# A Strassen unit in tile 1, two key selections side by side, and key sums behind the last values, in a fused attention and feed-forward kernel

## The chip, the core and the metric

One core of a Trainium2 chip. The metric is the device time of one execution in microseconds (us); a kernel is timed in several runs and the median is quoted. Ratios are computed as the mean time of one kernel's fast runs over the mean of the other's fast runs of the same rounds, so they are not quite the ratios of the medians. A run more than 1.5% above the fastest of its kernel counts as slow and is left out of the ratio. The span of a profile (first to last instruction) is about 1.8 us shorter than the timed execution that it belongs to.

Engines: PE is the tensor engine, DVE the vector engine, ACT the scalar engine, POOL is GpSimd, SP only issues transfers here. A *bank* is one of the eight result buffers that PE writes; before PE starts another result in it, this program lets it wait until DVE or ACT have read ("evicted") the old one.

## The reference, cut to what matters

```python
# q, k, v: (8 batches, 8 heads, 576, 64); 4608 tokens, 512 -> 2048 -> 512
k_p = k.reshape(B, H, 72, 8, D).mean(axis=3)        # pooled keys; values likewise
attn = softmax(q @ k_p.T / 8)
x = (attn @ v_p)                                    # to (4608, 512)
h = x @ w_in
out = (h * sigmoid(h)) @ w_out
```

## The kernel before

The kernel walks over nine tiles of 512 tokens. A tile has an *up* phase (x @ w_in and silu, hidden state transposed in `h_T`) and a *down* phase (the product with `w_out`). Attention for the next batch is cut into small pieces, *fillers*, hung between the matmuls: `f_up.append((22, f))` means that f is emitted after step 22 of the up phase. In the up phase a step is one matmul of 512 columns or a pair of 256.

The up phase has two kinds of work: a *plain* group (four matmuls of 512 columns and one activation), or a *unit*, Strassen's scheme for four groups at once: seven products of four 256-column matmuls, with sums on DVE.

```python
def product(y, n, bank, first):
    if first:
        ps[bank] = ps_tile([128, 2, NQ], FP32, "at", f"u_ps{bank}")   # pool "at": 5 banks, "mm": 3
    w, x = unit_weights(y, n), unit_x(t, n)
    ...                                             # 4 matmuls
def stage(y, n):
    if n == "2":   product(y, 2, "P", True);  nc.scalar.copy(r_sb, ps["P"])
    elif n == "5": product(y, 5, "Q", True);  tt(out=rr_sb, in0=ps["Q"], in1=r_sb, op=ALU.add)
    elif n == "1": product(y, 1, "R", True);  tt(out=t_sb, in0=ps["R"], in1=rr_sb, op=ALU.subtract)
    elif n == "4": product(y, 4, "P", False); hidden(y, 1, 0, ps["P"])
    elif n == "3": product(y, 3, "Q", False); hidden(y, 0, 1, ps["Q"])
    ...
```

The down phase is one such scheme for the whole tile. It needs sums of the hidden state (`hidden_sum`, on DVE) and ends with `o_sb` being evicted from banks P and Q:

```python
def down_quarters(t, fillers, last=False):
    product(2, KA, KQ); product(5, KA, KQ); product(2, 0, KA)      # 2 and 5 read hidden sums
    nc.scalar.copy(r_sb, ps["P"]); product(5, 0, KA)
    tt(out=rr_sb, in0=ps["Q"], in1=r_sb, op=add)
    ...                                             # products 1, 4, 3
    product(7, 0, KQ, cc); tt(out=o_sb[0][:, cs, LO], in0=ps["P"][:, cs], in1=t_sb[:, cs], op=add)
    product(6, 0, KQ, cc); tt(out=o_sb[1][:, cs, HI], in0=ps["Q"][:, cs], in1=t_sb[:, cs], op=add)
```

The attention pieces that the argument touches (shortened):

```python
def pool_k(b, stage):               # from batch 3 on; keys come in two transfers, the second adding
    if stage == 0: add_halves(raw)  # DVE, 72x1024: the first reader of the landed keys
    else: ...                       # DVE, two more sums, to kp
def select_k(b, a): ...             # 12 small PE matmuls into half a of one bank (batches 0 to 2)
def copy_k(b, a):                   # DVE copy of that half to kz
def select_v(b, a): ...             # PE;  copy_v(b, a): DVE copy of half a to vp
def numerators(b, g, f):
    ... lhsT=st["vp"][:, 4 * g + s, c::2] ...       # s in 0..3: half g of vp alone
    nc.vector.tensor_mul(out=xT[...], in0=nu[c], in1=rec)
```

Names in the profile lines: `kp` and `vp` are the pooled keys and values, `kz` the keys as PE reads them; `x_sum`, `w_sum` and `h_sum` are sums of inputs, weights and hidden state; `r_sb`, `rr_sb`, `t_sb` and `c_sb` are the partial sums of a Strassen scheme; `nu_ps` are the numerators.

The softmax here doesn't subtract the row's maximum and nothing guards it: scores larger than these inputs give would overflow.

## Time and profile before

| | before |
|---|---|
| median of the first runs | 294.97 us (294.23 to 295.34) |
| the profiled execution | 293.2 us, span 291.4 us |
| PE / DVE / ACT busy | 97% / 76% / 64% |

The lines are shown in the prediction below. How to read it: PE is busy all through, so time is gained by less work on PE or by fewer of PE's waits, and a wait on PE shows as a start later than the previous start plus 216 ns (512 columns) or 109 ns (256).

For the comparisons I cut the trace at PE's first matmul of each tile (the first `hp_ps` matmul after the last `o_ps` one; where its record is missing, 0.216 us before the next). In the profile before, tile 1 took 33.39 us, tile 2 29.96, tile 3 29.30, and tiles 4, 5, 6 30.31, 29.68 and 30.95.

### The profile page before, as it was taken

The page shows a single profiled execution, that of the slowest core. Times are in us where ns is not written, and L with a number is a line of the kernel's source. Part 1 is how long each engine was busy: PE and PEld are TensorE (multiplying, and loading weights), DVE is VectorE, ACT ScalarE, POOL GpSimd, SP SyncE. Part 2 cuts the span into 40 slices and gives each one's busy share as a digit, 9 for nine tenths or more (in the row PEclk, how much of TensorE's full clock was granted, in tenths as well). Part 3 has the DMA queues.
Part 4 walks back from the last instruction along what each step waited for, and adds up shares of the span by engine and source line. Part 5 has one row for each costly group of instructions (what it writes and reads, how often), then busy time and mean ns, then how long its engine had stood idle before and what let it go on. Part 6 is the DMA issues. An engine that isn't in the chain of part 4 may idle for free. (4 is left out here: it accounts for less than half of the span.)

```text
span 291.4 us, 6563 instructions
## 1 busy us (share of the span) xinstructions
PE 282.9 (97%) x2565; PEld 188.7 (65%) x2585; DVE 222.3 (76%) x408; ACT 187.4 (64%) x400; POOL 52.2 (18%) x68
## 2 busy tenths in 40 slices
PE   8989999989999999999999999999999999999995
PEld 3448434445667676667788767676666666786684
DVE  4986845964889697979598869987888876746783
ACT  1668675558666877588757866786578667425800
POOL 8754216501020012001200107103000000000000
PEclk9999999999999999999999999999999999999999
DMA  7999999993677463954894394978830023004104
GB/s 209 277 279 214 240 290 159 220 208 46 131 104 171 116 102 65 155 153 135 127 182 125 83 150 72 175 149 155 143 91 2 2 54 90 3 0 108 39 2 144
DMA packets 35295, 37.67 MB, mean 129 GB/s; under 512 B 9952, under 2 KB 27616, under 8 KB 35264
## 3 DMA queue, kind: packets, MB, share of 16 engines
q0 software_dynamic: 21760, 20.86, 42.4%
q1 hardware_dynamic: 12928, 15.48, 20.9%
q10 hardware_dynamic: 576, 0.92, 0.9%
q8 instruction: 20, 0.33, 0.5%
q14 instruction: 11, 0.09, 0.1%
HBM read 36.70 MB, written 9.44 MB: 158 GB/s over the span
## 5 line engine op out<-in xcount | busy, mean ns | idle before, releaser
L517 PE MATMUL hp_ps<-xT,w_in_sb 128*128 128x512 bf16 (+3 forms) x413 | 83.6, 340 | 1.9 <-DVE o_sb L653 0.6
L523 ACT ACTIVATE h_T<-hp_ps 128x512 bf16<-128x512 f32 (+2 forms) x99 | 53.7, 548 | 36.7 <-PE hp_ps L517 35.7
L622 PEld LDWEIGHTS <-h_sum 128*128 128x128 bf16 x640 | 60.4, 98 | 15.0 <-issue 6.1
L582 DVE TENSOR_TENSOR h_sum<-h_T 128x1024 bf16<-128x1024 bf16 (+1 forms) x72 | 50.9, 743 | 12.3 <-ACT h_T L523 12.3
L517 PEld LDWEIGHTS <-w_in_sb 128*128 128x128 bf16 x428 | 40.7, 98 | 28.1 <-issue 2.5
L338 ACT ACTIVATE es<-sc_ps 72x288 bf16<-72x288 f32 x128 | 41.3, 402 | 12.6 <-PE sc_ps L330 12.5
L378 DVE TENSOR_TENSOR xT<-nu_ps,rec 128x288 bf16<-128x288 f32 x64 | 25.5, 447 | 8.8 <-PE nu_ps L370 8.8
L459 PEld LDWEIGHTS <-w_sum 128*128 128x128 bf16 x280 | 27.3, 98 | 7.1
L622 PEld LDWEIGHTS <-h_T 128*128 128x128 bf16 x256 | 23.5, 98 | 6.8 <-issue 4.3
L467 ACT ACTIVATE h_T<-c_sb 128x512 bf16<-128x512 f32 x28 | 17.6, 628 | 10.4 <-DVE c_sb L491 10.4
L152 DVE STREAM_TRANSPOSE qT<-q_bf 128x576 bf16<-128x576 bf16 x32 | 23.0, 753 | 0.1
L181 POOL DMA_DIRECT2D raw<-in_k_dram x5 | 7.0, 1404 | 80.5 <-DMA raw<-in_k_dram 39.6
L356 ACT ACTIVATE lnd<-den_ps 128x288 f32<-128x288 f32 x30 | 12.3, 410 | 10.9 <-PE nu_ps L370 5.9
L273 DVE TENSOR_TENSOR raw<-raw 128x384 f32<-128x384 f32 (+3 forms) x20 | 12.4, 619 | 8.1 <-DMA raw<-in_v_dram 4.4
L622 PE MATMUL o_psP<-w_out_sb,h_sum 128*128 128x256 bf16 x128 | 17.6, 273 | 0.0
L622 PE MATMUL o_psQ<-w_out_sb,h_sum 128*128 128x256 bf16 x128 | 17.6, 273 | 0.0
L622 PE MATMUL o_psQ<-w_sum,h_T 128*128 128x256 bf16 x128 | 17.5, 274 | 0.0
L622 PE MATMUL o_psP<-w_sum,h_sum 128*128 128x256 bf16 x128 | 17.0, 273 | 0.0
L622 PE MATMUL o_psR<-w_sum,h_sum 128*128 128x256 bf16 x128 | 16.7, 273 | 0.0
L622 PE MATMUL o_psP<-w_sum,h_T 128*128 128x256 bf16 x128 | 16.7, 273 | 0.0
L187 DVE TENSOR_TENSOR raw<-raw 72x1024 f32<-72x1024 f32 x10 | 12.2, 1215 | 5.0 <-DMA raw<-in_k_dram 5.0
L529 POOL DMA_DIRECT2D out_dram<-o_sb x1 | 0.6, 626 | 83.5 <-issue 83.5
(77 smaller groups left out, 419.9 us busy)
## 6 DMA issues: line engine op xcount, KB each, us to landing
out_dram<-o_sb SPq DMA_DIRECT2D x128, 64.0 KB, 2.5
q_bf<-in_q_dram POOLq DMA_DIRECT2D x6, 576.0 KB, 10.7
raw<-in_k_dram SPq DMA_DIRECT2D x6, 512.0 KB, 5.2
raw<-in_k_dram POOLq DMA_DIRECT2D x5, 576.0 KB, 8.3
raw<-in_v_dram POOLq DMA_DIRECT2D x5, 576.0 KB, 8.6
raw<-in_v_dram SPq DMA_DIRECT2D x5, 512.0 KB, 5.7
w_in_sb<-in_moe_w_in_dram POOLq DMA_DIRECT2D x8, 256.0 KB, 8.6
w_out_sb<-in_moe_w_out_dram POOLq DMA_DIRECT2D x4, 512.0 KB, 13.4
```

Source lines behind the costliest of these rows:

```text
L152: nc.vector.transpose(out=st["qT"][:, a, f * QF : (f + 1) * QF].rearrange("r i c p -> r (i c p)"), in_=st["q_bf"][:, a, f * n : (f + 1) * n],)
L187: nc.vector.tensor_add(out=raw[:, :, : 2 * D], in0=raw[:, :, : 2 * D], in1=raw[:, :, 2 * D :])
L273: nc.vector.tensor_add(out=raw[..., :w], in0=raw[..., :w], in1=raw[..., w : 2 * w])
L338: nc.scalar.activation(es[:, s, :], sc[s], func=AF.Exp, scale=score_scale)
L356: nc.scalar.activation(lnd, den_ps[:, :HS], func=AF.Ln)
L378: nc.vector.tensor_mul(out=xT[:, 2 * g + c, cols], in0=nu[c][:, :HS], in1=rec)
L459: nc.tensor.matmul(ps[bank][:, u, :], lhsT=w[:, kk, 128 * u : 128 * (u + 1)], rhs=x[:, kk, :], start=first and u == 0 and kk == 0, stop=kk ...
L467: nc.scalar.activation(h_T[:, g : g + 2, j * NQ : (j + 1) * NQ], src, func=AF.Silu)
L517: nc.tensor.matmul(hp_ps[:, r0:r1], lhsT=w_in_sb[:, kk, g * 128 : (g + 1) * 128], rhs=xT[:, kk, x0 : x0 + r1 - r0], start=(kk == 0), stop= ...
L523: nc.scalar.activation(h_T[:, g, n0 : n0 + n], hp_ps[:, :n], func=AF.Silu)
L582: nc.vector.tensor_tensor(out=h_sum[n][:, ks, :], in0=quarter(*a, ks), in1=quarter(*b, ks), op=op)
L622: nc.tensor.matmul(ps[b][:, c, :], lhsT=left(n, kt, c), rhs=W_OUT[n][:, kt, :], start=b not in begun, stop=kt == k1 - 1, skip_group_check= ...
```

## The change

Its intent: (a) tile 1 gets one Strassen unit in place of four plain groups, with the weight and x sums moved to suit; (b) the two halves of the key selection of batch 2 stand side by side, with the two copies behind them, so that no selection waits for a copy; (c) the key sums of the next batch go behind the multiply of the last values; (d) bank R of the units moves to the pool of three.

```diff
--- before.py
+++ after.py
@@ -451,7 +451,8 @@
 
         def product(y, n, bank, first):
             if first:
-                ps[bank] = ps_tile([128, 2, NQ], FP32, "at", f"u_ps{bank}")
+                tag = "mm" if bank == "R" else "at"
+                ps[bank] = ps_tile([128, 2, NQ], FP32, tag, f"u_ps{bank}")
             w, x = unit_weights(y, n), unit_x(t, n)
             for u in range(2):
                 next(step)
@@ -768,18 +769,20 @@
         else:
             G = lambda *gs: [(g, 0, NTT) for g in gs]
             if t == 1:
-                items = G(*range(12, 16), *range(4, 12), *range(4))
+                items = (
+                    G(12, 13, 14, 15) + [(0, "251")] + G(8) + [(0, "43")] + G(9)
+                    + [(0, "76")] + G(10) + [(0, "s")] + G(11, 0, 1, 2, 3)
+                )
             else:
                 items = (
                     G(12, 13) + [(0, "251")] + G(14) + [(0, "43")] + G(15) + [(0, "76")]
                     + [(1, "2")] + [(0, "s")] + [(1, "51")] + G(0) + [(1, "43")] + G(1)
                     + [(1, "76")] + G(2) + [(1, "s")] + G(3)
                 )
-            if t > 1:
-                for n in U_X:
-                    f_up.append((0, lambda n=n: unit_x_sum(t, n)))
+            for n in U_X:
+                f_up.append((0, lambda n=n: unit_x_sum(t, n)))
             for n in (2, 5):
-                f_up.append((36, lambda n=n: hidden_sum(n, 4, 8)))
+                f_up.append((36 if t > 1 else 45, lambda n=n: hidden_sum(n, 4, 8)))
             f_up.append((56, lambda: hidden_sum(6, 4, 8)))
             for n, k0 in ((2, 0), (5, 0), (1, 4), (1, 0)):
                 f_up.append((64, lambda n=n, k0=k0: hidden_sum(n, k0, k0 + 4)))
@@ -788,14 +791,14 @@
 
         for n, t0, f_to, at, parts in (
             (1, 0, f_down, 48, (0, PW)), (3, 0, f_down, 52, (0, PW)),
-            (4, 1, f_up, 8, (0, PW)), (7, 1, f_up, 13, (0, PW)),
-            (6, 1, f_up, 40, (0, PW)),
+            (4, 1, f_up, 38, (0, PW)), (7, 1, f_up, 42, (0, PW)),
+            (6, 1, f_up, 60, (0, PW)),
         ):
             for i in range(*parts):
                 if t == t0:
                     f_to.append((at + i, lambda n=n, i=i: weight_sum(n, i)))
         if a < B:
-            q_at = [15, 16, 17, 49] if t else [82, 84, 86, 88]
+            q_at = [15, 16, 17, 49] if t > 1 else [24, 25, 26, 49] if t else [82, 84, 86, 88]
             if t == 0:
                 for j in range(2):
                     f_up.append((44 + 8 * j, lambda j=j: slot_sums("k", j)))
@@ -807,8 +810,8 @@
             elif t == 1:
                 for j in range(2):
                     f_up.append((0, lambda j=j: slot_sums("k", j, halves=True)))
-                    f_up.append((21 + 4 * j, lambda j=j: select_k(2, j)))
-                    f_up.append((21 + 4 * j, lambda j=j: copy_k(2, j)))
+                    f_up.append((22, lambda j=j: select_k(2, j)))
+                    f_up.append((23, lambda j=j: copy_k(2, j)))
                     f_down.append((8, lambda j=j: slot_sums("v", j, halves=True)))
                     f_down.append((40, lambda j=j: select_v(2, j, "at")))
                     f_down.append((41, lambda j=j: copy_v(2, j)))
@@ -828,8 +831,8 @@
                     for n in U_W:
                         f_down.append((6, lambda y=y, n=n: unit_weight_sum(y, n)))
             elif a + 1 < B:
-                f_down.append((80, lambda: pool_k(a + 1, 0)))
-                f_down.append((100, lambda: pool_k(a + 1, 1)))
+                for stage in range(2):
+                    f_down.append((100, lambda stage=stage: pool_k(a + 1, stage)))
                 f_up.append((0, lambda: load_q(a + 1)))
                 f_up.append((1, lambda: load_one(a + 1, "k")))
                 f_up.append((2, lambda: load_rest(a + 1, "k")))
```

## The prediction

> **What bounds the kernel now.** I read the page's busy shares first, then the chain that ended last, then the timelines of TensorE (PE) and VectorE (DVE) where the change acts.
>
> ```profile
> PE 282.9 (97%) x2565; PEld 188.7 (65%) x2585; DVE 222.3 (76%) x408; ACT 187.4 (64%) x400; POOL 52.2 (18%) x68
> ...
> 240.43 0.86 PE hp_ps L517 x4
> 241.29 0.44 PE u_psP L459 x4
> ```
>
> PE is the bound: the last 75 us of the chain hold almost nothing else. One plain group (hp_ps, four matmuls of 512 columns) costs 0.86 us, one product of a Strassen unit (u_ps, four of 256) 0.44. Only two things can gain: less PE work, or fewer PE waits. PE is busy by a modelled end, so I looked for waits as matmul starts further apart than 216 or 109 ns. Stretches of 216 ns in which a record is missing are not waits.
>
> The waits that the change can reach are these. In tile 1 (PE timeline, then DVE):
>
> ```profile
> 59.06 0.81 PE L517 MATMUL hp_ps<-xT,w_in_sb 128*128 128x512 bf16 x3 [0.16 <-issue]
> 60.78 0.64 PE L295 MATMUL kz_ps<-shifts,k 128*32 128x72 bf16 x12 [0.91 <-DVE kz L302]
> ...
> 59.11 1.42 DVE L152 STREAM_TRANSPOSE qT<-q_bf 128x576 bf16<-128x576 bf16 x2
> 60.47 0.27 DVE L302 CAST kz<-kz_ps 128x144 bf16<-128x144 f32 x1
> ...
> 70.39 2.50 DVE L582 TENSOR_TENSOR h_sum<-h_T 128x1024 bf16<-128x1024 bf16 x4 [3.67 <-ACT h_T L523]
> ...
> 76.26 0.74 DVE L320 CAST vp<-v_ps 72x256 bf16<-72x256 f32 x2
> ```
>
> The second key selection waits until DVE, busy with transposes, has copied the first out of the same bank. Later DVE is idle 3.67 us before the hidden sums of the down phase, so it has room here; from 70.39 to 77.00 it runs almost without a pause, and the numerators start at 77.17, right behind its copy of the values (vp).
>
> At the end of tile 3 (DVE, then PE):
>
> ```profile
> 142.40 0.69 DVE L649 COPY o_sb<-o_psQ 128x512 f32<-128x512 f32 x1 [0.28 <-PE o_psQ L622]
> 144.90 1.22 DVE L187 TENSOR_TENSOR raw<-raw 72x1024 f32<-72x1024 f32 x1 [1.81 <-DMA raw<-in_k_dram]
> 146.04 0.81 DVE L378 TENSOR_TENSOR xT<-nu_ps,rec 128x288 bf16<-128x288 f32 x2
> 146.77 0.68 DVE L653 TENSOR_TENSOR o_sb<-o_psP,t_sb 128x512 f32<-128x512 f32 x1
> 147.37 0.75 DVE L192 TENSOR_TENSOR kp<-raw 72x256 bf16<-72x256 f32 x2
> 148.04 0.68 DVE L657 TENSOR_TENSOR o_sb<-o_psQ,t_sb 128x512 f32<-128x512 f32 x1
> ...
> 147.50 1.03 PE L517 MATMUL hp_ps<-xT,w_in_sb 128*128 128x256 bf16 x8 [0.19 <-DVE o_sb L653]
> ...
> 155.56 0.60 PE L459 MATMUL u_psP<-x_sum,w_in_sb 128*128 128x256 bf16 x4
> 156.28 0.60 PE L459 MATMUL u_psQ<-x_sum,w_in_sb 128*128 128x256 bf16 x4
> ```
>
> The key sum (L187) waits 1.81 us for its transfer, and all of DVE with it: the values' multiply, ready since 144.0, and the eviction of bank P (L653). PE's second group of tile 4 wants that bank. From start-to-start distances PE loses here 0.35 us, then 0.05 and 0.29 where products of the units wait for rr_sb (155.56 to 156.28 is 0.72 instead of 0.44). The same distances give 0.15 after tile 4 and 0.57+0.07+0.29 = 0.93 after tile 5. After tiles 1 and 2, where the keys have long landed, they give nothing:
>
> ```profile
> 83.28 1.21 DVE L187 TENSOR_TENSOR raw<-raw 72x1024 f32<-72x1024 f32 x1
> 84.41 1.54 DVE L378 TENSOR_TENSOR xT<-nu_ps,rec 128x288 bf16<-128x288 f32 x4
> 85.87 0.67 DVE L653 TENSOR_TENSOR o_sb<-o_psP,t_sb 128x512 f32<-128x512 f32 x1
> 86.47 0.74 DVE L192 TENSOR_TENSOR kp<-raw 72x256 bf16<-72x256 f32 x2
> 87.22 0.69 DVE L657 TENSOR_TENSOR o_sb<-o_psQ,t_sb 128x512 f32<-128x512 f32 x1
> ```
>
> **What the Trainium skill says.** "TensorE: Matmul & The Clock Gate", section "Wait — 56ns, not 53.3ns?": warm matmuls start N / 2.4 GHz + about 2.5 ns apart; that is 216 and 109 ns, as the chain has it (0.86/4, 0.44/4). "PSUM — Partial Sum Buffer", "PSUM bank collisions raise a hardware error": guard by bank and quadrant, not by address; agrees with the 0.91 us, the halves having different columns. Its section "Engine vs sequencer instructions": VectorE's queue is strict FIFO; agrees with the multiply stuck behind L187. "VectorE: DVE Perf Modes", "The perf-mode tier table": a two-tensor operation has a doubled rate for bf16 in SBUF alone; here one x_sum of 512 columns costs 1.76/5 = 0.35 us, but the unit's sums out of PSUM 0.69.
>
> **The change, part by part.**
>
> (a) The Strassen unit in tile 1. On PE four plain groups go (4 x 0.864 = 3.45 us) and seven products come (7 x 0.437 = 3.06): saved 0.39. DVE gains five x_sums (1.76) and four fp32 sums (about 0.65 each, 2.6): 4.4 us. ScalarE trades four activations for four like them and a copy of 0.58: it has room.
>
> (b) The selections side by side. Before, the first took 0.53 us of PE over the matmuls it sits between (58.32 to 59.06 less one matmul), the second 1.43 with the wait. Together they should cost some 0.8 (one change of matmul shape less, no wait): saved 1.15.
>
> So PE's up phase of tile 1 falls from 15.93 us (53.63 to 69.56) by 1.55 to 14.4, ending at 68.0. Now DVE. Its queue: last multiply to 54.3, x_sums to 56.1, key slots (1.6) to 57.7. Then rr_sb waits for ScalarE's copy of P, which stands behind a table load and four activations (55.73 + 4 x 0.58 + 0.58 = 58.6). From 58.7 on DVE doesn't rest: rr_sb and t_sb 1.4, two key copies 0.55, three transposes 2.0, two c_sb 1.25, twelve weight sums 12 x 0.355 = 4.25, three hidden sums 1.95: together 11.4, to 70.0. The four last hidden sums start at 70.0, not at 70.39. PE wants the first at 68.0 + 2.25 = 70.25 and gets it at 70.7; then everything behind (values' slots, rr_sb, hidden sum 7, copy of vp) follows on DVE as before, only 0.4 earlier. So the numerators start at about 76.75 instead of 77.17. Of the 1.55 us, 0.4 arrives; 1.15 turns into PE waits on hidden sums and vp. From there PE bounds again.
>
> (c) Key sums behind the last values. In tiles 3 to 5 the multiply and L653 go ahead of the wait. After tile 3: multiply 144.1 to 144.9, L653 to 145.6, L187 to 146.8, L192 to 147.5, L657 to 148.1. Bank P is free in time (0.35 gone), and L657 ends 1.8 us after PE's start on tile 4 instead of 2.44. What a late L657 costs I read from the trace: 1.83 us cost 0.15 (tile 5), 2.09 (2.44 less the 0.35 that PE had waited) cost 0.34, 0.89 nothing: about its excess over 1.7. So some 0.1 is left of 0.69; the same working gives 1.7 for tile 4 (0.05 left of 0.15) and 1.75 for tile 5 (0.05 of 0.93). But after tiles 1 and 2 there was no wait to hide: L187 moves from DVE's free time into its rush. DVE then idles 83.36 to 84.2, multiplies to 85.95, L653 to 86.55, L187 to 87.7, L192 to 88.4, L657 to 89.0: 2.0 after PE's start, where it was 0.9. That costs 0.3 each. Balance: 1.77 - 0.2 - 0.6 = 0.95, say 0.9.
>
> (d) R in the other pool of banks. It takes the bank of Q that L657 frees; PE wants it 2.6 us after its start, L657 comes at 2.0. No gain, no loss.
>
> Sum: 0.4 + 0.9 = 1.3 us: 294.97 - 1.3 = 293.7.
>
> **The rivals.** First, PE's saving arrives whole: 1.55 + 1.77 = 3.3, so 291.6. For it speaks DVE's 76% share; against it that DVE's idle time in tile 1 lay mostly in one piece before the last hidden sums, and 4.4 us of work with a wait for ScalarE fill it. Second, DVE becomes the bound in tile 1: if the chain there is 1 us longer than I have it (a c_sb waiting for PE, weight sums slowed), the numerators come later than 77.17, tile 1 loses 0.5, and with 0.6 lost after tiles 1 and 2 the total stays near 294.5 to 295. Third, the key transfers: a later L192 frees the key buffer later. But the next load sits behind 16 stores on its queue and the first stores hang on L653, which doesn't get later; so I expect the landings to move with the kernel.
>
> **Range and chances.** 293.7; the three runs of before spread over 1.1 us, and tile 1 may be off by 0.7 either way: 292.4 to 295.0. Even the first rival is 1.1%, and 2% is 5.9 us: faster 0.02, within 2% 0.97, slower 0.01.
>
> **What the new profile should show.** No PE wait of a kz_ps on DVE kz; tile 1's up phase 14.4 us; DVE without idle from about 58.7 in tile 1; PE waiting about 0.4 for h_sum at the start of the down phase and about 0.7 for vp; in tiles 3 to 5 L653 before L187 and no PE wait for it; after tiles 1 and 2 new PE waits of about 0.3 on rr_sb. I am wrong if DVE shows idle stretches just before the last hidden sums of tile 1 (then its gain is 1 us more), if L187 at its new place still waits for its transfer, or if R waits for L657.

## The result, and the profile after

| | median us | lowest to highest | runs |
|---|---|---|---|
| before | 294.60 | 293.89 to 295.34 | 4 |
| after | 290.66 | 290.43 to 291.88 | 4 |

The ratio is 0.9874 (95% interval 0.9835 to 0.9914). The prediction was 293.7 with a range from 292.4 to 295.0: the time lies below the range. The class "within 2%" was right, but the gain is three times the one predicted, and beyond even that of my first rival, in which PE's saving arrives whole (291.6).

The two profiled executions differ by less, 291.4 to 288.6 us. The page of the changed kernel:

```profile
PE 281.2 (97%) x2578; PEld 189.9 (66%) x2597; DVE 226.8 (79%) x417; ACT 187.9 (65%) x401; POOL 52.2 (18%) x68
```

DVE has 4.5 us more work, as the prediction had it (4.4). Where the 2.8 us came from, tile by tile:

| tile | before | after | difference |
|---|---|---|---|
| until the first dense matmul | 17.19 | 17.05 | -0.14 |
| 0 | 36.44 | 36.45 | 0.01 |
| 1 | 33.39 | 32.02 | -1.37 |
| 2 | 29.96 | 30.10 | 0.14 |
| 3 | 29.30 | 29.63 | 0.33 |
| 4 | 30.31 | 29.62 | -0.69 |
| 5 | 29.68 | 29.54 | -0.14 |
| 6 | 30.95 | 30.00 | -0.95 |
| 7, 8 | 54.17 | 54.17 | 0.00 |

**Tile 1**, DVE of the changed kernel (start, duration, line, operation, out<-in, and in brackets the idle time before it with what ended it). Lines of the kernel have moved by one, so L654 here is L653 of before:

```profile
57.23 0.29 DVE L277 TENSOR_TENSOR k<-raw 128x128 bf16<-128x128 f32 x1
58.41 0.69 DVE L480 TENSOR_TENSOR rr_sb<-u_psQ,r_sb 128x512 f32<-128x512 f32 x1 [0.89 <-ACT r_sb L477]
...
68.18 1.43 DVE L601 TENSOR_TENSOR w_sum<-w_out_sb 128x512 bf16<-128x512 bf16 x4
69.52 2.49 DVE L583 TENSOR_TENSOR h_sum<-h_T 128x1024 bf16<-128x1024 bf16 x4
...
75.19 0.74 DVE L320 CAST vp<-v_ps 72x256 bf16<-72x256 f32 x2
```

and PE:

```profile
70.27 1.05 PE L623 MATMUL o_psP<-w_out_sb,h_sum 128*128 128x256 bf16 x8
...
75.46 0.27 PE L623 MATMUL o_psP<-w_sum,h_T 128*128 128x256 bf16 x1
75.66 0.43 PE L370 MATMUL nu_ps<-es,vp 72*32 72x288 bf16 x8
```

The DVE queue runs in the predicted order: it waits for ACT until 58.41, and then has next to no gap until the last hidden sums. But these start at 69.52 and not at 70.0, and the copies of vp end at 75.93, where 0.4 us before the 77.00 of the kernel before would be 76.6. The matmul at 70.27 starts 0.20 us late for the hidden sums. And the numerators start at 75.66, while the second copy of vp ends only at 75.93 (75.19 + 0.74): they don't need it. In the kernel before, the first copy had ended by 76.67 and the numerators came at 77.17, 0.20 after the product before them, as in all such changes of matmul shape in the two traces (0.201 to 0.204). So there was slack, and I had read a wait.

**The end of tile 3**, DVE after:

```profile
142.91 0.82 DVE L378 TENSOR_TENSOR xT<-nu_ps,rec 128x288 bf16<-128x288 f32 x2 [0.86 <-PE nu_ps L370]
143.70 0.69 DVE L654 TENSOR_TENSOR o_sb<-o_psP,t_sb 128x512 f32<-128x512 f32 x1
144.31 1.21 DVE L187 TENSOR_TENSOR raw<-raw 72x1024 f32<-72x1024 f32 x1
...
146.23 0.68 DVE L658 TENSOR_TENSOR o_sb<-o_psQ,t_sb 128x512 f32<-128x512 f32 x1
```

The multiply and the eviction of P now go ahead of the key sum L187, which finds its data landed. L658 ends at 146.91, 1.66 us after PE's start on tile 4 (145.25), where the prediction had 1.8. PE starts the second group without a wait:

```profile
145.25 1.91 PE L518 MATMUL hp_ps<-xT,w_in_sb 128*128 128x256 bf16 x16
```

**Tile 2**, PE after; here the change costs, as predicted. The second line starts 0.73 after the first where 0.44 is the rule; it waits for rr_sb, which ended at 95.05:

```profile
94.38 0.60 PE L460 MATMUL u_psP<-x_sum,w_in_sb 128*128 128x256 bf16 x4
95.11 0.60 PE L460 MATMUL u_psQ<-x_sum,w_in_sb 128*128 128x256 bf16 x4
```

Two questions are left. Is the slack at vp the whole reason for tile 1's extra microsecond? And where do the timed runs get another 0.3 to 1.1 us that the two traces don't show?

### The profile page after: what moved, and what is told of

Its sections match the earlier page's. It is cut to its first block, busy times and chain, and to the rows that moved or that the text cites. A ratio compares the mean times of both kernels' runs of the same rounds, so it can differ in the third digit from the quotient of the medians.

```text
span 288.6 us, 6600 instructions
## 1 busy us (share of the span) xinstructions
PE 281.2 (97%) x2578; PEld 189.9 (66%) x2597; DVE 226.8 (79%) x417; ACT 187.9 (65%) x401; POOL 52.2 (18%) x68
## 4 chain that ended last, share of the span: by engine, by line
PE 91%; DVE 2%; ACT 2%; DMA 2%; issue 1%; DVEq 0%
PE hp_ps L518 24%; PE o_psP L623 15%; PE o_psQ L623 15%; PE u_psQ L460 6%; PE u_psP L460 6%; PE o_psR L623 5%; PE o_ps L550 4%; PE sc_ps L330 4%; PE nu_ps L370 3%; PE den_ps L347 3%; PE u_psR L460 2%; DMA raw<-in_k_dram 2%; PE warm_ps L672 1%; ACT es L338 1%; PE kz_ps L295 1%
## 5 line engine op out<-in xcount | busy, mean ns | idle before, releaser
L518 PE MATMUL hp_ps<-xT,w_in_sb 128*128 128x512 bf16 (+3 forms) x398 | 80.5, 338 | 1.2 <-ACT h_T L524 0.4
L524 ACT ACTIVATE h_T<-hp_ps 128x512 bf16<-128x512 f32 (+2 forms) x95 | 51.4, 545 | 33.1 <-PE hp_ps L518 31.9
L518 PEld LDWEIGHTS <-w_in_sb 128*128 128x128 bf16 x412 | 39.3, 98 | 24.9 <-issue 1.5
L460 PEld LDWEIGHTS <-w_sum 128*128 128x128 bf16 x300 | 29.3, 98 | 7.7
L468 ACT ACTIVATE h_T<-c_sb 128x512 bf16<-128x512 f32 x30 | 18.8, 628 | 10.8 <-DVE c_sb L492 10.8
L623 PE MATMUL o_psQ<-w_sum,h_sum 128*128 128x256 bf16 x128 | 15.4, 273 | 0.0
## 6 DMA issues: line engine op xcount, KB each, us to landing
q_bf<-in_q_dram POOLq DMA_DIRECT2D x6, 576.0 KB, 11.4
```

The source lines that it names most:

```text
L460: nc.tensor.matmul(ps[bank][:, u, :], lhsT=w[:, kk, 128 * u : 128 * (u + 1)], rhs=x[:, kk, :], start=first and u == 0 and kk == 0, stop=kk ...
L468: nc.scalar.activation(h_T[:, g : g + 2, j * NQ : (j + 1) * NQ], src, func=AF.Silu)
L518: nc.tensor.matmul(hp_ps[:, r0:r1], lhsT=w_in_sb[:, kk, g * 128 : (g + 1) * 128], rhs=xT[:, kk, x0 : x0 + r1 - r0], start=(kk == 0), stop= ...
L524: nc.scalar.activation(h_T[:, g, n0 : n0 + n], hp_ps[:, :n], func=AF.Silu)
L623: nc.tensor.matmul(ps[b][:, c, :], lhsT=left(n, kt, c), rhs=W_OUT[n][:, kt, :], start=b not in begun, stop=kt == k1 - 1, skip_group_check= ...
```

## The experiments

In each diff, `-` is the kernel named, `+` the experiment. All ratios lie within 2% of 1 and most of their intervals overlap, so what is small is read from the tiles of the traces.

### The parts alone

**e1**: the changed kernel again, in the same rounds as e2 to e4.

> The changed kernel again, timed in the same rounds as the parts below. The two profiled executions differ by 2.8 us (291.4 to 288.6), the timed medians by 3.9. Theory T (the traces tell all): the ratio is 0.9905, 2.8 us, and the rest was the spread of the runs of before. Rival V (a part of the gain comes and goes with the transfers, and the profiled execution of before was a lucky one): the ratio stays near 0.987, 3.7 us, and the spans of before show more than 291.4 in most rounds.

**e2**: before, with part (c) alone.

```diff
-                f_down.append((80, lambda: pool_k(a + 1, 0)))
-                f_down.append((100, lambda: pool_k(a + 1, 1)))
+                for stage in range(2):
+                    f_down.append((100, lambda stage=stage: pool_k(a + 1, stage)))
```

> The kernel before with the key sums alone moved behind the last values. Theory T: gains 0.69 + 0.14 + 0.95 at the ends of tiles 3, 4, 5 and loses 0.3 to 0.35 each at tiles 1 and 2: 1.1 us, ratio 0.996. The prediction on record: 0.9, ratio 0.997. Rival V (the waits for the keys' transfers are often longer than in the profiled execution of before): 2 us or more, ratio 0.993 or less.

**e3**: before, with part (b) alone.

```diff
-                    f_up.append((21 + 4 * j, lambda j=j: select_k(2, j)))
-                    f_up.append((21 + 4 * j, lambda j=j: copy_k(2, j)))
+                    f_up.append((22, lambda j=j: select_k(2, j)))
+                    f_up.append((23, lambda j=j: copy_k(2, j)))
```

> The kernel before with the two key selections of batch 2 side by side and nothing else. DVE keeps its idle time in tile 1, so both the prediction on record and theory T say 1.15 us, ratio 0.996, with tile 1's up phase 14.8 us instead of 15.9. If the first selection was not really waiting for the copy, nothing.

**e4**: the changed kernel with the edits of e2 and e3 undone, so parts (a) and (d).

> The unit in tile 1 with its moved weight sums and transposes and the other pool for R, but the selections apart and the key sums where they were. PE has 0.39 us less work. Theory T: the second selection still waits for a copy, now behind rr_sb and t_sb (to about 60.4 us, a wait of 1 us or more), so the gain is 0.2 to 0.4 us, ratio 0.999. Rival (the extra 4.4 us of DVE in tile 1 cost more than they bring): slower by 0.3 us or more, ratio over 1.001.

| | median us | lowest to highest | ratio | tile 1 | tiles 2, 3 | tiles 4 to 6 |
|---|---|---|---|---|---|---|
| before | 293.93 | 293.35 to 296.74 | | 33.39 | 59.26 | 90.94 |
| e1 all | 290.81 | 290.73 to 291.33 | 0.9882 | 32.01 | 59.73 | 89.16 |
| e2 (c) | 292.83 | 292.22 to 293.09 | 0.9945 | 33.40 | 59.94 | 89.17 |
| e3 (b) | 293.04 | 292.63 to 293.86 | 0.9959 | 32.19 | 59.25 | 91.23 |
| e4 (a, d) | 292.43 | 291.82 to 292.97 | 0.9933 | 32.70 | 59.06 | 90.64 |

(The tiles of before are those of its first profile.) What follows:

- e2 confirms the arithmetic of (c) in the trace: 0.34 and 0.33 lost in tiles 2 and 3, 1.78 won in tiles 4 to 6. The median moves by 1.1; the ratio says 1.6, because the longest runs of before count in its mean. Rival V wanted 2 us or more: the median speaks against it, the interval (0.9911 to 0.9979) holds both.
- e3: tile 1 wins 1.20, as both theories had it (1.15). But tiles 4 to 6 take 0.3 us *more* than in the profile before.
- e4: the unit wins 0.69 in tile 1, more than the 0.2 to 0.4 I expected. Its wait for a key copy is 0.41 instead of 0.91 us (the copies stand behind rr_sb and t_sb, but PE comes later too). That halved wait is also why (a) and (b) don't add: 0.69 + 1.20 against 1.37 together.
- e1: the timed gain of the whole change is 3.1 us by the medians, near theory T's 2.8, and 3.5 by the ratio, near rival V's 3.7; the interval (0.9845 to 0.9919) holds both, so e1 does not decide. The kernel before spreads over 3.4 us (1.7 without the run at clock 0.994), the changed one over 0.6.

### What is lost with the early key sums, and a version without the loss

**e5**: the changed kernel without (c): `- for stage in range(2): ... 100` back to `80` and `100`.

> The changed kernel with the key sums back where they were (the unit and the selections alone). Theory E (eaten): before the last values DVE waits for the keys' transfer at the end of tile 3, and that transfer does not come earlier by as much as the kernel does (with the selections alone it landed 0.6 us earlier where PE was 1.2 us ahead, and tile 4's start lost 0.56 more). So of the 1.4 + 0.2 us won in tiles 1 and 2 about 0.6 is lost again at tile 4, and the gain is 1.0 to 1.3 us, 292.7. Theory S (the parts simply add): 3.1 of the whole change less 1.1 of the key sums, 2.0 us, 291.9, with tile 4 no longer than the 30.5 us of the kernel before.

Measured: median 292.35 us (291.27 to 297.12) against 294.29 (292.87 to 295.90), ratio 0.9926. Tile 4 took 30.17 us, no longer than in before, so theory E (a part of the gain is eaten at the end of tile 3) isn't seen here. The median lies between the two forecasts; without the slow run (297.12, at clock 0.994) it is 291.66, beside theory S. The 0.6 us that e3 had lost in tile 4 was one draw, not a rule.

**e6**: the changed kernel, key sums late in tiles 3 to 5 alone.

```diff
-                for stage in range(2):
-                    f_down.append((100, lambda stage=stage: pool_k(a + 1, stage)))
+                f_down.append((80 if t < 3 else 100, lambda: pool_k(a + 1, 0)))
+                f_down.append((100, lambda: pool_k(a + 1, 1)))
```

> The changed kernel, but the key sum goes behind the last values in tiles 3, 4 and 5 alone; in tiles 1 and 2, where its transfer has long landed, it stays early. By the prediction's reading, which e2 confirmed (0.34 and 0.33 lost at the starts of tiles 2 and 3), both losses go: 0.65 us faster than the changed kernel, ratio 0.986, tiles 2 and 3 with up phases of 13.15. If the later landing of the next keys takes it back, nothing.

Measured: median 290.39 us (290.00 to 293.03), ratio 0.9880. In the trace both losses are gone: tiles 2 and 3 together 59.05 us against 59.73, tiles 4 to 6 89.15. By the clock it is 0.4 us below e1, on another chip, so the trace carries this and the time does not.

**e7**: the changed kernel with R back in the pool of five (`tag = "at"`).

> The changed kernel with bank R of the units back in the pool of five. The prediction says no gain and no loss. Rival: the 0.2 us that tile 2's down phase lost in the kernel before (16.81 against 16.61) is a wait for a bank that R held, so it returns, and tile 1 may lose as well: 0.2 to 0.5 us slower than the changed kernel.

Measured: median 290.80 us (290.48 to 292.45), ratio 0.9883: as the changed kernel. The rival fell: tile 2's down phase stayed at 16.61. Its profile fell on its slowest run, 292.45 us, and shows that the key sum can still wait at its new place, one of the prediction's signs of being wrong, which the first profile did not show. DVE at the end of tile 3:

```profile
144.72 0.69 DVE L653 TENSOR_TENSOR o_sb<-o_psP,t_sb 128x512 f32<-128x512 f32 x1
146.11 1.22 DVE L187 TENSOR_TENSOR raw<-raw 72x1024 f32<-72x1024 f32 x1 [0.70 <-DMA raw<-in_k_dram]
```

Here tiles 4 to 6 took 90.20 us instead of 89.16. The eviction of P is safe in front of the wait, the eviction of Q and the x sums behind it are not.

**e8**: e6, and weight sum 6 of tile 1 moved into the down phase.

```diff
-            (6, 1, f_up, 60, (0, PW)),
+            (6, 1, f_down, 50, (0, PW)),
```

> As e6, and the four parts of weight sum 6 of tile 1 (1.43 us of DVE just ahead of the last hidden sums) move into the down phase at step 50. If DVE's queue sets the hidden sums' start, they come earlier and PE's wait of 0.2 us for them at the start of the down phase goes: 0.2 us faster than e6, tile 1 31.8. If the wait is for the last activation instead, nothing; if the sums disturb the down phase, slower.

Measured: tile 1 31.81 us instead of 32.01, as expected: DVE's queue, not the last activation, set that start, and PE's 0.2 us wait is gone. The profiled execution is the shortest so far (289.64 us, span 287.8). But the median was 291.24 (289.64 to 291.71), ratio 0.9886. Timed again below (e15).

### The slack at the values

**e9** and **e10**: one line doubled, in before and in the changed kernel. The result is the same, DVE has 1.2 us more just ahead of the copies of vp.

```diff
             f_down.append((33, lambda: hidden_sum(7, 0, 8)))
+            if t == 1:
+                f_down.append((33, lambda: hidden_sum(7, 0, 8)))
```

> The kernel before with hidden sum 7 of tile 1 computed twice: 1.2 us more of DVE just ahead of the copies of vp, so a reading of how much slack PE had there. The prediction on record read the numerators (77.17 us) as released by vp, with none: tile 1 grows by 1.2 us. The new reading: the first numerators need only the first of the two copies, ended at 76.68, and PE came at 77.0 to 77.2 by its own work: slack 0.5, so tile 1 grows by 0.7 us (33.39 to 34.1).

> The same in the changed kernel, where the first copy of vp ends at 75.61 and the numerators start at 75.66. New reading: the slack is used up, so nearly all of the 1.2 us shows: tile 1 grows by 1.1 to 1.2 us (32.02 to 33.2). If the numerators still came by PE's own work with room to spare, less.

Measured: (one execution each, so only the tiles are read) tile 1 grew from 33.39 to 34.20 in before (0.81) and from 32.02 to 33.26 in the changed kernel (1.24). The lines that decide it, first e9 (before), DVE and PE:

```profile
78.16 0.75 DVE L320 CAST vp<-v_ps 72x256 bf16<-72x256 f32 x2
...
78.63 0.43 PE L370 MATMUL nu_ps<-es,vp 72*32 72x288 bf16 x8 [0.74 <-DVE vp L320]
```

then e10 (after):

```profile
77.38 0.74 DVE L320 CAST vp<-v_ps 72x256 bf16<-72x256 f32 x2
...
77.85 0.43 PE L370 MATMUL nu_ps<-es,vp 72*32 72x288 bf16 x8 [1.19 <-DVE vp L320]
```

In both, the numerators start 0.47 us after the start of the two copies and well before their end: they wait for the first copy alone. The 1.21 us of added work cost 0.81 in before, so PE had 0.4 us of slack there; in the changed kernel they cost all, so the slack is used up. The prediction's reading, no slack before, would have made it 1.2 in both.

### What differs from run to run

**e11**: before, with R in the other pool alone.

> The kernel before with bank R of the units in the pool of three and nothing else. The prediction says nothing changes. What e4 to e6 suggest (they have R there and tile 2's down phase of 16.61 instead of 16.81): tile 2 is 0.2 us shorter, and no other tile changes but for the keys' transfer.

Measured: 293.24 us in one run; tile 2 29.96, unchanged. The prediction's "no gain, no loss" for (d) stands, and what I had made of e4 to e6 (that R shortens tile 2) was wrong.

**e12**: before, unchanged, for a second trace.

> The kernel before, unchanged, for a second trace of it: its timed runs spread from 292.9 to 296.7, those of the changed kernel hardly at all. Theory V (the waits for the keys' transfer at the ends of tiles 3 to 5 differ from run to run): tiles 4, 5, 6 differ from 30.53, 29.68, 30.95 by some tenths each way, all other tiles are the same to 0.05 us, and a slow run has the longest of them. Rival (the first microseconds, before the first dense matmul, make the spread): those three tiles repeat and the start differs from 17.19 us.

Measured: 295.1 us in one run, at full clock, span 293.3. Against the first trace of the same kernel: 0.69 us more until the first dense matmul, and 0.11, 1.19, -0.11 in tiles 4, 5, 6; all other tiles the same. Both the theory and the rival have a share, 1.2 and 0.7 of 1.9 us. DVE at the end of tile 4, and PE at the start of tile 5:

```profile
176.59 1.22 DVE L187 TENSOR_TENSOR raw<-raw 72x1024 f32<-72x1024 f32 x1 [2.40 <-DMA raw<-in_k_dram]
...
179.19 1.02 PE L517 MATMUL hp_ps<-xT,w_in_sb 128*128 128x512 bf16 x4 [0.79 <-DVE o_sb L653]
```

In the first trace that L187 had waited 1.22 us. The view of waits sums them up (waiting engine and line, releaser, total, times, longest). First trace of before:

```profile
DVE raw L187 <- DMA raw<-in_k_dram: 5.0, 3, 2.0
```

second trace:

```profile
DVE raw L187 <- DMA raw<-in_k_dram: 6.2, 3, 2.4
```

In the first profile of the changed kernel, and in those of e6 and e8, that view has no such line.

**e13**: before, with the first half of the keys on another queue. In the kernel before this load is on SP's queue, behind the sixteen stores of the last tile.

```diff
-        load_rows(nc.sync, raw, source(b, name)[:, :, :PH])
+        load_rows(nc.gpsimd if name == "k" else nc.sync, raw, source(b, name)[:, :, :PH])
```

> The kernel before with one change: the first half of the keys is loaded on GpSimd's queue, where it does not stand behind the sixteen stores, so the keys should land some 8 us or more earlier, while the key sum stays ahead of the last values. Theory V (the time that moving the key sums wins, and the spread of the kernel before, are both DVE waiting for this transfer): L187 waits nowhere, tiles 4, 5, 6 fall from 30.5, 29.7, 30.9 to about 29.3 to 30.0 without the 0.3 us losses at tiles 2 and 3, the profiled span is near 289.6, the median 1.8 to 3 us below the kernel before, and the timed runs keep within about 1 us. Rival (the place of the key sum among DVE's instructions is what counts, whatever it waits for): no gain, and the spread stays.

Measured: median 292.16 us, lowest 291.97, highest 292.41, against 294.65 (292.79 to 297.40), ratio 0.9923 (0.9897 to 0.9949). Nothing on DVE waits for these keys, with the key sum still in its *old* place. DVE at the end of tile 3:

```profile
143.31 1.21 DVE L187 TENSOR_TENSOR raw<-raw 72x1024 f32<-72x1024 f32 x1
144.44 0.81 DVE L378 TENSOR_TENSOR xT<-nu_ps,rec 128x288 bf16<-128x288 f32 x2
145.17 0.68 DVE L653 TENSOR_TENSOR o_sb<-o_psP,t_sb 128x512 f32<-128x512 f32 x1
```

Tiles 4 to 6 take 89.17 us, as in the changed kernel, and the spread has shrunk from 2.6 us (292.79 to 295.38, the fast runs of before) to 0.4. So the rival (the place of the sum is what counts) is out: what (c) takes away is a wait for a transfer, and in these rounds this wait is most of what made the kernel before uneven. The median fell by 2.5 us (2.3 by the ratio), though 0.5 were lost in tile 8 (29.38 instead of 28.88).

**e14**: e8 with the load of e13. **e15**: e8 again, in the same rounds.

> e8 with the keys loaded early as in e13. Theory V: e8's profile has no wait for keys, but its timed runs spread over 2 us; with the landing far ahead they keep within 1 us, median about 289.7, the lowest so far. Rival (the spread of e8 is something else, the start or the chip): as e8, 289.6 to 291.7.

> e8 again, on the same chip and in the same rounds as e14. Its tiles add up to 0.9 us less than those of the changed kernel; timed on another chip it was no faster. Theory: 0.9 us faster than the changed kernel's 290.7, 289.8; rival: it stays at 291, and the difference to its profile is a wait that comes and goes.

| | median us | lowest to highest | ratio | tile 1 | tiles 4 to 6 |
|---|---|---|---|---|---|
| before | 294.65 | 292.79 to 297.40 | | | |
| e14 | 290.25 | 290.07 to 290.40 | 0.9858 | 31.80 | 89.16 |
| e15 | 290.10 | 289.67 to 290.96 | 0.9858 | 31.81 | 89.48 |

e14 is the most even of all (0.3 us), but at 290.25 not the 289.7 that I expected. Of the 0.5 us between its trace and that of e8, 0.14 is in tile 8 (29.02 against 28.88) and 0.34 before the first dense matmul (17.51 against 17.17). e15's profile again holds a wait of 0.25 us for the keys, at the end of tile 5. Both ratios are lower than the changed kernel's 0.9874 and 0.9882, but the intervals overlap (0.9835 to 0.9881, 0.9832 to 0.9884), and e8, the same kernel as e15, first had 0.9886: a small further gain, likely and not proven.

## Why the prediction was wrong, point by point

**Right.** The up phase of tile 1 fell to 14.35 us (14.4 predicted); the two selections together (e3: 1.20 in tile 1, 1.15 predicted); DVE as the limit for the last hidden sums of tile 1 (e8: with 1.4 us less ahead of them PE's wait goes); the order at the ends of tiles 3 to 5; the losses in tiles 2 and 3 (0.34 and 0.33 against "0.3 each"); nothing from R.

**Wrong: "the numerators start at about 76.75 instead of 77.17. Of the 1.55 us, 0.4 arrives; 1.15 turns into PE waits on hidden sums and vp".** This is the step that failed, DVE's path to the numerators of tile 1. In the profile after they start at 75.66, PE waits 0.20 us for the hidden sums and no measurable time for vp, and 1.37 us arrive. Two terms of the path were off:

- DVE's queue was summed too long. Its wait for ACT ended at 58.41 instead of 58.7 (0.13 of this because all of tile 1 starts earlier), the work from there to the last hidden sums took 11.1 us instead of 11.4, and from these to the end of the copies of vp 6.4 instead of the 6.6 of the kernel before.
- The numerators were taken to be released by both copies of vp. They read one half of vp and start after the first copy (e9, e10, and 75.66 against 75.93 in the profile after). By e9 the kernel before had 0.4 us of slack there, which the change could use up. The evidence was at hand: the half that the numerators index stands in the code, and the 0.20 us ahead of them is the same as ahead of the denominators, which wait for no copy.

An estimate from these ends: had the numerators needed both copies, they would have started at 75.99 (0.06 after the copy's end, as in e9 and e10), and 1.04 us would have arrived. So of the 0.97 us that the prediction missed in tile 1, the queue is about 0.6 and the second copy about 0.3. The sign that I had named for such a miss, idle stretches of DVE just before the last hidden sums, did not come: the queue was full, and only shorter than I had it.

**Less far off than the time suggests: part (c).** The prediction wanted 0.9. In the traces (c) alone (e2) wins 1.78 in tiles 4 to 6 and loses 0.7 in tiles 2 and 3, 1.1 in all. The wait was read from one execution, and it differs from run to run: over the undisturbed 89.16 us, tiles 4 to 6 took 1.8 us more in the first trace, 3.0 in the second (30.41 + 30.87 + 30.84 = 92.12), and 1.4 to 2.5 in the five other traces with the sum at its early place (e3, e4, e5, e9, e11). The first is the median of these seven, so the term was not read from a lucky execution.

**Not asked:** why the profiled execution of before (293.2 us) was 1.8 us faster than the median that I subtracted from (294.97). In the traces tiles 1 to 3 give 0.9 us and tiles 4 to 6 1.8 (3.0 against the second trace), together 2.7 to 3.9. The timed gains, 3.7 us by the first ratio (2.5 to 4.9) and 3.5 by e1's (2.4 to 4.6), hold this range. The time until the first dense matmul, 17.1 to 18.1 us, moves single runs by as much. How much of the timed gain above 2.7 us is a longer wait for keys and how much is chance isn't shown, since a trace exists for one execution of each run alone.

**A slip without effect:** 0.35 us is the share of one in five overlapping x_sums, 0.69 the length of one sum out of PSUM; like for like (`--lines`) one operation takes 0.42 and 0.69.

**The third rival**, that the landings move with the kernel, was argued too simply. In e3 PE was 1.2 us ahead at the end of tile 3, and the keys landed 0.6 earlier; in e5 they landed 1.7 earlier with PE 1.6 ahead. The landing has a scatter of its own.

**Left open.** Tile 2's down phase is 0.2 us shorter (16.61) in every kernel with the unit in tile 1, and in e13. In before, e2, e3, e9, e11 and e12 one `c_sb` of tile 2 waits 0.60 us (0.43 in e2) for an activation of a plain group, whose output it doesn't read; in e13 a wait of the same size sits in tile 8, beside the 0.5 us lost there; no kernel with the unit has it in either place. R isn't its cause (e11, e7); what is, no run here settles. Nor do I know what makes the keys' transfer take longer in one run than in another.

## What to carry to other kernels

Compare the profiled execution with the timed median before subtracting anything, and take a few more traces before giving a wait for a transfer a size: here it was 1.4 to 3.0 us in seven of them. An instruction that waits for a transfer on an in-order engine takes everything behind it along, so put it behind the work that frees a bank, or issue the load where it does not stand behind stores. And before you call a consumer released by a producer, look which part of the buffer it reads, and whether it starts right behind the producer or right behind its own engine's work.

## What the Trainium skill lacked or had wrong

- "DMA: Bandwidth & Descriptors", "Anatomy of one DMA — SWDGE (gpsimd) path", fits 2.0 us plus the bytes at 436 GB/s; an estimate from it for the keys' second transfer (576 KB) is 2.0 + 0.59 MB / 436 GB/s = 3.4 us. Here the fifteen of these transfers in three traces (the two of the kernel before, and e11) took 7.5 to 11.2 us from issue to landing, beside other transfers and adding to their target. I found there no time for an adding transfer beside others, nor for the scatter from run to run.
- No page says how far the waits of one profiled execution may differ from those of the next: 1.8 and 3.0 us in the same three tiles of the same kernel here.
- No page has a wait like that of `c_sb` for an activation that it doesn't read (0.60 us, moving from tile 2 to tile 8 with an unrelated edit); it may be of the program rather than of the chip.
